# Three instruction orders written anew: a second attention core, the way to it, and a second convolution

## The chip, the core and the metric

The kernel runs on one core of a Trainium2 chip. The core has engines that work side by side, each through its own queue of instructions in order: TensorE (PE in the profile, its weight loads PEld), VectorE (DVE), ScalarE (ACT), GpSimd (POOL), and SyncE (SP), which here issues DMAs. They wait for each other by semaphores. The metric is the device time of one execution in microseconds; the time of a kernel is the median over its runs.

## The reference

Four layers act on x, of 2048 positions by 512 channels, each as x + f(layernorm(x)): A, B, A, B, with the same weights both times.

```python
def _A_ref(x, wqkv, wo):              # H = 32 heads of 16; window W = 8, dilation 2
    qkv = ... x @ wqkv ...
    idx = pos[:, None] - off[None, :]                  # off = 0, 2, .., 14
    logits = einsum("bhsd,bhswd->bhsw", q, kg) * scale # kg, vg: k and v at idx
    logits = where(mask, logits, -1e9)
    o = einsum("bhsw,bhswd->bhsd", softmax(logits), vg)
    return o.reshape(B, S, D) @ wo

def _B_ref(u, ...):                   # S4: a long convolution per channel
    P = exp(dt * A * l);  K = einsum("dn,dnl,dn->dl", Cc, P, dB).real
    y = irfft(rfft(pad(u)) * rfft(pad(K)))[:L]
    return y + u * Dskip
```

A is attention in which each position sees itself and seven others, at distances 2 to 14. B convolves each channel with a kernel K of full length, which is worked out from the parameters.

## The kernel before, in words

Position p*16 + a lies in partition p, row a: x is held as 128 partitions by 16 rows by 512 channels, so a distance of 2 positions is mostly a step of two rows, and a block b is four rows. The kernel goes through six stretches. The first (ORDERK, `k_gen`) works out K's table and, beside it, the first layer's norm and projections. The second is the first attention core (CORE0), the third the first convolution (ORDER0). Then come the three whose orders change: ORDERF, the end of the first convolution with the norm and the projections of the second A layer; CORE1, the second attention core; ORDER1, the second convolution.

What sets the order: the orders are strings written out by hand. Each token calls a function that records the instructions of one step on several engines. Under `manual_schedule`, TensorE, VectorE, ScalarE and SyncE get their instructions in the order of the tokens (DMAs of the ring loads are placed by the framework among SyncE's others). A token that stands earlier therefore stands earlier in the queue of each engine that it uses, and nothing overtakes it there.

The steps that the change and the prediction speak of:

* `differ(k)` (L1122 and on) ends a squaring of a table on TensorE: two matmuls in float32, each of two passes (L1129, L1130), that wait for ScalarE's squares `ws`. For k = 8, 9, 10 it first issues SQ_FILL[k] idle matmuls (L1128).
* ORDERF: `h` takes statistics of half a row on VectorE (L150), `H` of whole rows (L1553), `a` aggregates them (L1558), `p` makes 1/sqrt on ScalarE (L155, L156), `n` normalises a block of four rows (L197; D on VectorE, G half on GpSimd), `T` transposes it on TensorE (L273) into two halves that `E` copies out (L275; A on ScalarE, D on VectorE). `P` is one of 16 projections for k (four matmuls, L284, and ScalarE's copy L287), `Q` one for q (L223, L225). `x` and `e` copy a shifted part of k on VectorE (L297). `y`/`Y` (`i1`, in halves L901 or whole L897), `z`, `w` and `v` are the last steps of the convolution; `w` is 8 rows by 128 channels, `v` and `z` four rows. With the letter A ScalarE copies the sum of a `w`, `v` or `z` out and TensorE adds x by a matmul with the identity; with D VectorE adds x itself (L950). `S` gives half of the sums' buffers in PSUM to the projections.
* CORE1: `m` multiplies q by the windowed k for one of four parts ft of a block (`prod`, L344, VectorE; two buffers), `l` sums it over the channels of each head on TensorE (L352 for the first two blocks, L356 for the others), `x` takes the maximum, `e` subtracts it and takes the exponential, `r` the reciprocal of the sum, `n` normalises, `T` turns the first two blocks. `q` and `v` are projections (L223, L400). `P` multiplies a row's weights by v (`pav`, L469, VectorE; two buffers), `S` or `V` sums over the window on TensorE (L494, L484) and ScalarE copies the result (`oT`), `p` loads x into a PSUM buffer ahead (L501, ScalarE), `O` is the output projection (L511), with ScalarE's copy back to x and its sums for the next norm. `b` and `d` prepare that norm, `a` and `f` apply it to a row on VectorE or ScalarE. v is written row by row, even rows first; after v14 and v15 SyncE copies the even and the odd rows, shifted, for the windows (L405, L406). `w` loads a quarter of a table of the convolution.
* ORDER1: `U` is a first transform of u (TensorE, copied by VectorE or ScalarE, `a1s`), `u` a second one (ScalarE's copy `ub`, three buffers), `m` the product with the spectrum of K (VectorE, L871), `y`, `w` and `v` as above. A store of four rows (L1601) is issued when their last step is recorded.

In what follows m00 is token m of block 0, part 0; P0, S0, O0 are those of row 0; u14 is the fifteenth u, and so on.

Of the kernel before, what the change touches and what calls it, by code (L numbers as in the profile page):

```python
# [21 lines left out]
S = 2048  # L22
# [33 lines left out]
w010D  # L56
"""
ORDERF = """
yA h00 YA h01 v100A v110D h10 a0 z12A p0 z11A n0D h11 w001A w011A S a1 p1 T0 E01A z13A E00D n1G H2
P02 a2 P00 Q00 p2 T1 E10D E11D P01 P11 P12 n2D H3 a3 P13 T2 P10 E20D E21D P03 p3 P21 P22 n3D P23 T3  # L60
E30D E31A P20 x1
"""
ORDER1 = """
UA UD UA UD UA UA UD UA UD UD u u m m u u m m UA u UA UD m UA u u UD UA u m m u u m m u YD m u YA YA
m u yD m yA u u m m u w001A m m yA yA w000D YA yD yA YD w011D yA yD w010D yA yD yA v101A v103D v113A
v102D v112D v111D v110A v100A
"""

CORE0 = """
# [1 line left out]
nVPBeSOPSCd6wOPSwrPPnOSOSPPOSOPSbO9bFwEPAwVGaafOdSttDfOaHafa  # L71
"""
CORE1 = """
0mv12m3llmmqqqlqvlvmmvxvllmvevqrmvnllqqTvvmmlqlxmmvPPvvvvveqlmlqxmqSrnOSTpPPOlSeSrPOSOPSPPOSqlpO
SpmmOlOplnpPSxPeObbPdrpwVffaSfdOOPnVPPpfSpOSPpObafPSwOtppSdfwafwtaOa
"""
ROWS0 = (0, 2, 1, 3, 4, 5, 6, 7, 8, 9, 10, 11, 12, 13, 14, 15)
ROWS1 = (0, 2, 1, 3, 4, 5, 6, 7, 8, 9, 10, 11, 12, 13, 14, 15)
# [929 lines left out]
CH = 32  # L1008
NROW = 641
SQ_PE = 3  # L1010
SQ_FILL = {8: 13, 9: 6, 10: 2}


def k_gen(tc, nc, a_consts, ins, kd, la, x_v, lnst, zero, b_consts):
# [3 lines left out]
    with ExitStack() as ctx:  # L1018
# [102 lines left out]
        def differ(k):  # L1121
# [4 lines left out]
            re = pst.tile([P, 4 * P], F32, name="pt")  # L1126
            for _ in range(SQ_FILL.get(k, 0)):
                nc.tensor.matmul(re[:, 0:P], lhsT=ident32[:], rhs=nident32[:], start=True, stop=True)  # L1128
# [509 lines left out]
```

## Time and profile before

| | us |
|---|---|
| median of 3 runs | 397.38 (396.81 to 397.64) |
| profiled execution | 397.28 |
| its span | 395.5 |

| engine | busy us | share of the span |
|---|---|---|
| DVE | 377.5 | 95% |
| PE | 345.2 | 87% |
| ACT | 332.8 | 84% |
| PEld | 240.0 | 61% |
| POOL | 52.0 | 13% |

The profile is of one execution. A row of the timeline gives the start of a group of instructions in microseconds from the start of the span, its length, the engine, the line and the operation, the tile written and those read, the shapes and the count; in brackets stands how long the engine had been idle and what released it. A row of the chain gives start, length and what ran. A row by stretch gives, for each engine, its busy microseconds in the stretch, then TensorE's granted clock as a share of full speed, and the DMA engines' share and rate. The stretches: the way to the second core is about 235 to 263 us, the second core 261 to 350, the second convolution 350 to 392, then the last store.

### The profile page before, as it was taken

To read this page: it belongs to the slowest core of one execution; us is meant where nothing else is said; L and a number is where in the kernel's file an instruction comes from. 1 tells how busy PE (TensorE), PEld (TensorE's weight loads), DVE (VectorE), ACT (ScalarE), POOL (GpSimd) and SP (SyncE) were. 2 spreads that over 40 slices of the span, in tenths; PEclk is the share of its full clock that TensorE was granted. 3 is DMA by queue.
4 is the path that set the end of the run, shared out by engine and by line. 5 is a ranking of instruction groups with operands and counts; after the bars stand their busy time and mean duration, and the time that the engine had idled before them with its cause. 6 is when DMAs were issued, how large, how long until landed. Compare 5 with 4: busy or idle time off the path is not lost.

```text
span 395.5 us, 14987 instructions
## 1 busy us (share of the span) xinstructions
PE 345.2 (87%) x6551; PEld 240.0 (61%) x6598; DVE 377.5 (95%) x453; ACT 332.8 (84%) x594; POOL 52.0 (13%) x109
## 2 busy tenths in 40 slices
PE   3867667799999999889997889999999998887995
PEld 2225335485645677657887788543456666566885
DVE  6999999999999999999999989989999999989994
ACT  7999999899568789989999986674666899989974
POOL 9400100000370001002643500100000001000000
PEclk9999899999999999999999999999999999999999
DMA  7953811214125756394473907810153039505506
GB/s 224 388 159 41 80 53 32 64 29 92 53 50 144 196 169 179 97 364 169 166 247 125 323 15 209 317 58 0 49 153 95 3 106 325 163 2 163 162 10 207
DMA packets 63184, 54.17 MB, mean 137 GB/s; under 512 B 33035, under 2 KB 49968, under 8 KB 62864
## 3 DMA queue, kind: packets, MB, share of 16 engines
q1 hardware_dynamic: 60680, 46.60, 40.3%
q0 software_dynamic: 2432, 6.62, 4.7%
q8 instruction: 51, 0.84, 0.9%
q14 instruction: 13, 0.11, 0.1%
q10 hardware_dynamic: 8, 0.00, 0.0%
HBM read 30.15 MB, written 13.24 MB: 110 GB/s over the span
## 4 chain that ended last, share of the span: by engine, by line
DVE 35%; PE 33%; ACT 14%; issue 9%; DMA 6%; SPq 1%; POOL 1%; DVEq 0%; ACTq 0%; POOLq 0%
DVE pav L469 9%; PE pq L400 6%; DVE A_t L1161 4%; ACT a1s L814 4%; DVE prod L344 4%; DVE t L871 4%; PE pk L1327 4%; PE pq L223 3%; PE pp L284 3%; PE pp L1265 2%; DVE B_t L1161 2%; PE pq L511 2%; PE L L352 2%; PE po L494 2%; DMA pow_t<-pow_t 2%
## 5 line engine op out<-in xcount | busy, mean ns | idle before, releaser
L469 DVE TENSOR_TENSOR pav<-attn,v_ext 128x4096 bf16<-128x4096 bf16 (+1 forms) x34 | 72.0, 2163 | 0.3
L344 DVE TENSOR_TENSOR prod<-qT,kT_ext 128x4096 bf16<-128x4096 bf16 x29 | 65.2, 2288 | 0.7 <-PE L L352 0.5
L1161 DVE TENSOR_TENSOR A_t<-A_t,pow_t 128x1024 bf16<-128x1024 bf16 (+4 forms) x46 | 38.0, 872 | 0.4
L494 PEld LDWEIGHTS <-pav 64*128 64x128 bf16 x1664 | 26.5, 95 | 14.0 <-DVE pav L469 7.2
L494 PE MATMUL po<-ident,pav 64*128 64x64 bf16 x1664 | 29.1, 190 | 4.5 <-ACT oT L486 1.8
L511 PE MATMUL pq<-wop,oT 128*128 128x512 bf16 x113 | 30.7, 380 | 2.7 <-issue 1.3
L883 ACT CAST ub<-pb 128x1024 bf16<-128x1024 f32 x32 | 31.8, 1098 | 1.0 <-PE pb L832 1.0
L832 PE MATMUL pb<-a1s,w_sb 128*128 128x64 bf16 x768 | 27.8, 193 | 5.1 <-ACT ub L883 1.8
L400 PE MATMUL pq<-wv,xnT 128*128 128x512 bf16 x122 | 29.8, 379 | 0.2
L832 PEld LDWEIGHTS <-w_sb 128*128 128x128 bf16 x768 | 24.9, 98 | 7.7 <-issue 6.0
L814 ACT CAST a1s<-pb 128x1024 bf16<-128x1024 f32 x29 | 28.1, 1063 | 1.1 <-PE pb L825 1.1
L1265 PE MATMUL pp<-xnT,kT_ext 128*128 128x512 bf16 x88 | 23.0, 379 | 6.7 <-ACT xnT L1258 3.5
L402 ACT CAST v_ext<-pq 128x512 bf16<-128x512 f32 x32 | 18.6, 586 | 12.1 <-PE pq L400 11.9
L225 ACT CAST qT<-pq 128x512 bf16<-128x512 f32 x24 | 14.0, 584 | 12.8 <-PE pq L223 12.8
L1327 PE MATMUL pk<-B_t,A_t 128*64 128x84 bf16 (+1 forms) x512 | 23.3, 201 | 1.6 <-ACT kgs L1335 1.6
L1327 PEld LDWEIGHTS <-A_t 128*64 128x64 bf16 (+1 forms) x512 | 21.5, 103 | 5.3 <-issue 2.2
L814 DVE CAST a1s<-pb 128x1024 bf16<-128x1024 f32 x19 | 22.5, 1219 | 1.5 <-PE pb L825 1.4
L223 PE MATMUL pq<-xnT,kT_ext 128*128 128x512 bf16 x89 | 23.4, 380 | 0.4
L400 PEld LDWEIGHTS <-xnT 128*128 128x128 bf16 x128 | 11.7, 98 | 13.6 <-issue 1.3
L511 PEld LDWEIGHTS <-oT 128*128 128x128 bf16 x128 | 11.5, 98 | 12.7 <-ACT oT L496 2.2
L825 PE MATMUL pb<-F1c,xnT 128*64 128x128 bf16 x256 | 17.3, 219 | 1.9 <-ACT a1s L814 0.7
L1265 PEld LDWEIGHTS <-kT_ext 128*128 128x128 bf16 x96 | 8.5, 97 | 16.2 <-issue 8.4
(285 smaller groups left out, 918.2 us busy)
## 6 DMA issues: line engine op xcount, KB each, us to landing
w_sb<-w_dram SPq DMA_DIRECT2D x32, 256.0 KB, 5.6
w_dram<-xnT SPq DMA_DIRECT2D x1, 4096.0 KB
kf_ring<-kf_dram SPq DMA_DIRECT2D x13, 256.0 KB, 4.0
kf_ring<-kf_dram SPq DMA_DIRECT2D x26, 128.0 KB, 4.0
v_ext<-v_ext SPq DMA_DIRECT2D x4, 784.0 KB, 6.1
x_blk<-in_A_x_dram SPq DMA_DIRECT2D x4, 512.0 KB, 4.9
kT_ext<-in_A_wqkv_dram SPq DMA_DIRECT2D x4, 512.0 KB, 9.5
x_sb<-in_A_x_dram SPq DMA_DIRECT2D x4, 512.0 KB, 6.5
```

Of the source, the lines that this page charges most:

```text
L223: nc.tensor.matmul(pq[:], lhsT=self.wqk[:, dt, ft * P:(ft + 1) * P], rhs=self.xnT[:, dt, q * 512:(q + 1) * 512], start=(dt == 0), stop=(dt ...
L344: nc.vector.tensor_tensor(pr, self.qT[q][:, ft].unsqueeze(1).to_broadcast([P, W, 4, P]), kap, ALU.mult)
L400: nc.tensor.matmul(pp[:], lhsT=xnT[:, dt, a * P:(a + 1) * P], rhs=wv[:, dt, :], start=(dt == 0), stop=(dt == NDT - 1))
L469: nc.vector.tensor_tensor(pv[:, i], attn[:, n % 4].unsqueeze(2).to_broadcast([P, W, DH // parts, H]), vap, ALU.mult)
L494: nc.tensor.matmul(po[:, h, 0, i * nt + ft, :], lhsT=pvf[rows, i, w, ft * P:(ft + 1) * P], rhs=ident[rows, rows], start=(w == 0 and ft + i ...
L511: nc.tensor.matmul(pw[:], lhsT=oT[:, ftp, :], rhs=self.wo[:, ftp, :], start=False, stop=(ftp == NDT - 1), skip_group_check=ahead)
L814: (self.nc.scalar.copy if eng == "act" else self.nc.vector.tensor_copy)(dst, src)
L832: nc.tensor.matmul(p2[:, j, :], lhsT=self.w2[:, ec * EC + j, :], rhs=a1s[:, ec * EC + j, :], start=True, stop=True)
L883: nc.scalar.copy(ub[:], p2)
L1161: return lambda: nc.vector.tensor_tensor(*args)
L1265: nc.tensor.matmul(pps[kind, b, ft][:], lhsT=la.wqk[:, dt, c:c + P], rhs=la.xnT[:, dt, b * 512:(b + 1) * 512], start=(dt == 0), stop=(dt = ...
L1327: nc.tensor.matmul(o, lhsT=lhs, rhs=Bt[:, ri, c * CH + ql].rearrange("p b g -> p (b g)"), start=(not half and j % 4 == 0 and ri == 0), sto ...
```

## The change

Three strings are replaced and three numbers. ORDERF and CORE1 hold the same tokens as before in another order. In ORDER1, beside the order, w000 is copied out by ScalarE and no longer by VectorE (w000A for w000D), the last of the steps y, y15, is done in the whole form (Y), and the last steps v come in another order. SQ_FILL gets one idle matmul more for k = 8, two more for k = 9 and one more for k = 10.

```diff
 ORDERF = """
-yA h00 YA h01 v100A v110D h10 a0 z12A p0 z11A n0D h11 w001A w011A S a1 p1 T0 E01A z13A E00D n1G H2
-P02 a2 P00 Q00 p2 T1 E10D E11D P01 P11 P12 n2D H3 a3 P13 T2 P10 E20D E21D P03 p3 P21 P22 n3D P23 T3
-E30D E31A P20 x1
+yA YA h00 v100A h01 v110D h10 a0 z11A p0 w011A h11 n0D a1 z12A p1 S w001A T0 E01A z13A E00D P00 n1G
+H2 a2 P03 T1 Q00 E11D E10D p2 n2D P02 P01 H3 P10 P13 a3 P11 p3 T2 P12 E20D E21D n3D P23 P20 T3 E31A
+P22 x1 E30D P21
 """
 ORDER1 = """
-UA UD UA UD UA UA UD UA UD UD u u m m u u m m UA u UA UD m UA u u UD UA u m m u u m m u YD m u YA YA
-m u yD m yA u u m m u w001A m m yA yA w000D YA yD yA YD w011D yA yD w010D yA yD yA v101A v103D v113A
-v102D v112D v111D v110A v100A
+UA UD UA UD UA UA UD UA UD UD u u u UA UA m m UD UA u m UD u u UA m m u m m u u m m u u u YD YA m m
+YA u u yD m m yA yA yA u u m m m YA w000A w001A w010D yD yA YD yA yD yA yD YA w011D v101A v111D
+v102D v103D v113A v112D v110A v100A
 """
 CORE1 = """
-0mv12m3llmmqqqlqvlvmmvxvllmvevqrmvnllqqTvvmmlqlxmmvPPvvvvveqlmlqxmqSrnOSTpPPOlSeSrPOSOPSPPOSqlpO
-SpmmOlOplnpPSxPeObbPdrpwVffaSfdOOPnVPPpfSpOSPpObafPSwOtppSdfwafwtaOa
+0ml2vv1mmllq3mqqlvqqqmmxllmmevvrvvllnmmvqTvvlqxvlvvmmvPvvPellxrnqqqSTemmqSPOlPSOPSPOSOSPmOrpplSO
+OmbPndppllSfPxfOPSafebOVrPPppSOndpVwwfOPPSpOSpPbaOPfSdOppttSfafaaOww
 """
-SQ_FILL = {8: 13, 9: 6, 10: 2}
+SQ_FILL = {8: 14, 9: 8, 10: 3}
```

## The prediction

> **What bounds the kernel now.** I read the busy times by stretch first, then the chain that ended last, then the timelines of VectorE, ScalarE and TensorE in the second half, since the three orders act only behind 235 us.
>
> ```profile
> core 0: us, PE busy (x) PEld busy (x) DVE busy (x) ACT busy (x) POOL busy (x), PEclk, DMA share, GB/s
> ...
> 246.00:270.00 24.00, 23.45 (x155) 11.94 (x157) 21.41 (x45) 15.90 (x30) 1.68 (x2) 1.00 0.44 154
> 270.00:300.00 30.00, 29.73 (x296) 15.03 (x299) 30.00 (x16) 17.19 (x30) 0.00 (x0) 1.00 0.32 87
> 300.00:345.00 45.00, 40.55 (x1182) 28.99 (x1193) 44.51 (x38) 40.68 (x97) 1.04 (x1) 1.00 0.42 136
> ...
> 355.00:375.00 20.00, 16.35 (x470) 15.20 (x470) 19.87 (x18) 19.02 (x22) 0.00 (x0) 1.00 0.53 160
> 375.00:395.50 20.50, 15.42 (x470) 14.63 (x466) 15.35 (x16) 12.32 (x15) 0.00 (x0) 0.96 0.36 106
> ```
>
> The reader sees full engines: TensorE 23.45 of 24 us on the way to the second core, TensorE and VectorE together in that core's first half, VectorE in its second half with ScalarE close behind, VectorE and ScalarE in the convolution. The work stays the same but for one block, so an order can only take away the few waits that are left, or add some. The execution took 397.28 us, 1.78 around its span of 395.5; the median of the runs, 397.38, lies 0.1 higher. The sum is made against 397.28. About 0.2% (0.8 us) is what a measurement of this kernel can tell from no change.
>
> **Idle matmuls (SQ_FILL).**
>
> ```profile
> 30.60 3.06 PE L1128 MATMUL pt<-nident,ident 128*128 128x128 f32 x26
> 35.24 1.12 PE L1129 MATMUL pt<-ws,ident 128*128 128x512 f32 x2 [1.58 <-ACT ws L1114]
> ...
> 37.06 1.50 PE L1128 MATMUL pt<-nident,ident 128*128 128x128 f32 x12
> 41.38 1.27 PE L1129 MATMUL pt<-ws,ident 128*128 128x512 f32 x2 [2.81 <-ACT ws L1114]
> ...
> 44.15 1.06 PE L1128 MATMUL pt<-nident,ident 128*128 128x128 f32 x4
> 45.53 1.16 PE L1129 MATMUL pt<-ws,ident 128*128 128x512 f32 x2 [0.32 <-ACT ws L1114]
> ```
>
> ```profile
> 43.88 0.58 ACT L1149 CAST B_t<-pt 128x512 bf16<-128x512 f32 x1
> ```
>
> Thirteen calls are 26 passes in 3.06 us, 0.235 us each. One more at k=8 goes into a wait of 1.58 us, two more at k=9 (0.47) into one of 2.81. One more at k=10 takes 0.24 to 0.5 us of a wait of 0.32, so at most 0.2 sticks out, and the matmuls behind it feed copies that stand behind other ScalarE work. I take 0; bounds -0.3 and +0.2.
> Behind the wait of 2.81 us the matmuls are slow: the four passes from 41.38 are through at 44.15, in 2.77 us, those from 35.24 were through at 37.06, in 1.82. A shorter wait (2.34) could keep the clock up and give TensorE 0.95 us; but the reader of its result, ScalarE, is in its own queue until 43.88 and beyond, so I count nothing of it. The Trainium skill ("TensorE: Matmul & The Clock Gate", Part 1) has the clock halved after one idle window of some 3.4 us. Here it fell after 2.81 us with little work before, so the trace bears the rule out only roughly; by it the shorter wait would be safe, and that is the fourth case below.
>
> **The way to the second core (ORDERF).** The same 54 tokens in another order. Their price is when the first product (token m00, line 344) can start.
>
> ```profile
> 241.74 0.41 DVE L1558 BATCH_NORM_AGGREGATE ln_ag<-ln_bn 128x2 f32<-128x12 f32 x4
> ...
> 242.86 1.38 DVE L197 TENSOR_SCALAR xn<-x_sb,ln_rstd,ln_nb 128x512 bf16<-128x512 bf16 x4
> 244.15 1.40 DVE L150 BATCH_NORM_STATS2 ln_bn<-x_sb 128x6 f32<-128x256 bf16 x4
> ...
> 261.88 1.10 DVE L297 COPY kT_ext<-kT_ext 128x2032 bf16<-128x2032 bf16 x2 [0.35 <-ACT kT_ext L287]
> 263.02 2.29 DVE L344 TENSOR_TENSOR prod<-qT,kT_ext 128x4096 bf16<-128x4096 bf16 x1
> ...
> 268.68 8.90 DVE L344 TENSOR_TENSOR prod<-qT,kT_ext 128x4096 bf16<-128x4096 bf16 x4 [0.51 <-PE L L352]
> ```
>
> ```profile
> 246.26 1.00 ACT L275 COPY xnT<-pt 128x1024 bf16<-128x1024 bf16 x1
> ```
>
> ```profile
> 259.13 1.18 PE L273 MATMUL pt<-ident,xn 128*128 128x128 bf16 x16
> 260.14 3.40 PE L284 MATMUL pp<-xnT,kT_ext 128*128 128x512 bf16 x15
> ```
>
> ```profile
> 250.63 3.45 PE pp L284 x16
> ```
>
> h11, a set of statistics, now stands ahead of n0D on VectorE. a0 ends at 242.15, h11 takes 1.35, so the four normalisations of n0D end at 245.0, not 244.24; a1 ends at 245.3 and ScalarE's p1 at 245.75. Behind p1 ScalarE now has w001A's copy (0.95) before E01A, so E01A, the second half of the transposed block, runs 246.6 to 247.6, 0.35 later than in the row. TensorE is on T0 and z13A until 247.15, then on P00 (16 matmuls in 3.45 us, so 0.86 for a group of four), whose last two matmuls find E01A done. Before, it stood for E01A; so at P00 it has lost only some 0.15. Two small waits are new: P23 for E21D, 0.15 (p2 stands behind Q00's copy, which moves n2D, H3 and E21D back), and T3 for n3D, 0.1. P30 ended two groups after 260.14, at 261.87; now at about 262.2. P22 and P21 come between T3 and P30 and cover E30D and E31A. x2 waits for P21's copy at 262.0, e0 for P30's at 262.8, and m00 starts at about 263.2: **+0.15**. Bounds: 0, and +0.6 if E01A's whole delay and both waits count.
>
> **The second core (CORE1).** From m00 to 349.6 VectorE had one wait, the 0.51 us ahead of m02. l00 now follows m00 at once, so m02 finds its buffer free and this wait goes. In exchange other products wait for a buffer. From m00 to m20 VectorE has eight products of 2.2, 0.7 of small copies, a maximum (1.13) and n0 (0.6): 20.0 us, to 283.2. TensorE from P30 to l12 has 19 groups of 0.86, seven half sums of 0.49 and 1.3 of small ones and waits, 21.1, to 283.4. So m20 waits 0.2. In the same way m23 waits 0.15 for l21, and m30 0.15 for q30's copy. With the 0.15 of the start and without the 0.51, P0 starts at about 293.55, where it did, and P1 at 304.3 for 304.1:
>
> ```profile
> 268.08 0.98 PE L L352 x16
> ```
>
> ```profile
> 293.56 4.50 DVE L469 TENSOR_TENSOR pav<-attn,v_ext 128x4096 bf16<-128x4096 bf16 x2
> ...
> 304.10 13.30 DVE L469 TENSOR_TENSOR pav<-attn,v_ext 128x4096 bf16<-128x4096 bf16 x6
> ```
>
> ```profile
> L405 SPq DMA_DIRECT2D v_ext<-v_ext x2: 657/668/678, 283.6 to 296.3; - x2
> ...
> DMA to landing us min/median/max: 5.8/6.0/6.2
> ```
>
> **+0.2 so far**; bounds -0.35 (no new wait) and +0.9. v14 moves back: TensorE is through it at 284.9, so the two shifted copies of v issue at 285.5 and 286.2, not from 283.6, and land by 292.3. P0's slack falls from some 3 us to 1.2. On SyncE a further ring load (two transfers) now stands ahead of them; it has nothing to wait for.
> At the core's end ScalarE counts as much as VectorE:
>
> ```profile
> 324.88 1.09 ACT L501 CAST pq<-x_sb 128x512 f32<-128x512 bf16 x2
> ...
> 348.85 0.80 ACT L195 ACTIVATE xnT<-x_sb,ln_nb,ln_rstd 128x512 bf16<-128x512 bf16 x1
> ```
>
> ```profile
> 349.18 0.42 DVE L197 TENSOR_SCALAR xnT<-x_sb,ln_rstd,ln_nb 128x512 bf16<-128x512 bf16 x1
> ```
>
> Both end at 349.6. In the new order ScalarE is through p7 and p8 at about 322.8, and S7, behind P7 on VectorE, gives it oT7 only at 323.9: 1.05 us idle. b1's root waits for P9 on VectorE, 0.25 more. Before, at 325.97, it had done oT7, O7 and p9 too, 2.4 us of work; now that is done by 326.5. Part is caught up in later gaps: I add **+0.2**, bounds 0 and +1.3 (both waits in full).
>
> **The second convolution (ORDER1).** w000 goes from VectorE to ScalarE, with eight matmuls by the identity (0.45 us); y15 takes the whole form, 0.4 more on TensorE.
>
> ```profile
> 355.81 3.76 ACT L883 CAST ub<-pb 128x1024 bf16<-128x1024 f32 x4 [0.71 <-PE pb L832]
> ...
> 378.24 2.87 ACT L814 CAST xnT<-pb 128x1024 bf16<-128x1024 f32 x3
> ...
> 390.71 1.25 ACT L952 CAST x_sb<-pb 128x512 bf16<-128x512 f32 x2 [1.43 <-PE pb L948]
> ```
>
> ```profile
> 379.66 1.22 DVE L950 TENSOR_TENSOR x_sb<-pb,x_sb 128x1024 bf16<-128x1024 f32 x1
> ```
>
> ```profile
> 230.06 1.04 PE pb L901 x64
> 231.10 1.00 PE pb L897 x16
> ```
>
> From 355.81 to 381.1 ScalarE has 27 copies almost without a pause, 0.93 each. In the new order yA4, yA5 and yA6 stand ahead of u14 and u15, so u14 is its 24th and ends at 378.05, when VectorE has been through m13 since 377.3. m14 waits 0.75, and m15 ends at 380.35, not at 379.66. w010D cannot start before TensorE has passed w000A and w001A (24 matmuls, 1.4 us each), at 381.1: VectorE waits again. From y7 (376.3, behind yA5's copy) TensorE has one piece of 15.1 us: w000, w001, y7, y10 and y15 in the whole form (0.93), six in halves (0.52), w010, w011 and the eight last (1.1 a pair). It ends at 391.4, and v100A's copy at 392.05 against 391.96: **+0.1**. The block VectorE no longer has (1.13) is eaten by its two waits. Bounds: -1.1 (they vanish) and +0.7 (m15's shift reaches the end).
>
> **The stores.** w011D moves behind y15, so the two stores of rows 8 to 15 issue at about 388.3.
>
> ```profile
> 392.00:393.00 1.00, 0.00 (x0) 0.00 (x0) 0.00 (x0) 0.00 (x0) 0.00 (x0) 1.00 1.12 335
> ```
>
> ```profile
> L1601 SPq DMA_DIRECT2D out_dram<-x_sb x8: 372/373/1439, 384.4 to 392.0; - x8
> ...
> DMA to landing us min/median/max: 2.2/2.4/3.3
> ```
>
> Six stores of 262 KB then move from about 389.5. At 335 GB/s, the best row, that is 4.7 us, to 394.2, just when the last one (392.0 and 2.2) landed; at 300 it is 5.2. I add **+0.3**, bounds 0 and +1.
>
> **Sum**: 0 + 0.2 + 0.2 + 0.1 + 0.3 = +0.8, so 397.28 + 0.8 = 398.1.
>
> **Rivals.** Faster: VectorE bounds the convolution, with a block less. It decides if u14's copy ends before 377.3. Then -1.1 in place of +0.1 and no delay of the stores: 397.28 + 0.4 - 1.1 = 396.6, or 396.2 without the core's 0.4. For it: ScalarE is idle late (1.43 before 390.71). Against: the wait lies earlier, where it is full.
> Slower: ScalarE sets the end of the second core and catches nothing up. It decides once O7's statistics and p9 end later than 326.5. +1.3 in place of +0.2 is 399.2; 399.9 with the stores at their upper bound. For it: 40.68 of 45 busy. Against: up to 322.8 it has done some 0.7 us more than it had before. The shifted copies of v, should they land behind 293.55, would cost the same way, microsecond by microsecond; 1.2 us of slack speaks against it.
> Fourth: the added fills do keep the clock up between 42 and 46 us, and 0.3 of that arrives: 397.8.
>
> **How the numbers follow.** Forecast (+0.8; its own range 397.3 to 398.9) 0.50; slower 0.24; faster 0.21; fourth 0.05. Of the forecast's case some 0.20 lies beyond 398.2, 0.2% over the median, so slower is 0.24 + 0.20 = 0.44. Below 396.6 lies most of the faster case, 0.19. The rest, 0.37, is no change. The range goes from the faster case's 396.3 to the slower one's 399.7.
>
> **What would show it.** Right: m00 at 263.1 to 263.6; no wait ahead of m02; P1 near 304.3; ScalarE waiting about 1 us for S7 near 323; VectorE waiting near 378 (m14) and 380.5 (w010D); TensorE without a gap from 376 to 391; the last store landing behind 394.2. Wrong: VectorE unbroken until w010D, which is the faster case; a wait ahead of P0; any shift of VectorE before 60 us, which would come from the fills.

## The result and the profile after

The changed kernel takes 399.62 us (median of 6 runs, 398.67 to 401.59) against 397.20 (6 runs, 396.31 to 397.64). The ratio is 1.0068, with a 95% interval of 1.0049 to 1.0087, or +1.9 to +3.5 us. The forecast was 398.1, +0.8: the sign is right, but the loss is about three times the size.

The profiled execution took 399.53 us, with a span of 397.4; before it took 397.28, with 395.5. So 1.9 of its 2.25 us lie in the span, which the views show. The other 0.35 lie outside it: time less span is 2.07 to 2.16 in the six runs of the changed kernel and 2.06 to 2.15 in the six with its three orders alone, but 1.73 to 1.90 in those of the kernel before, and 1.74 to 1.90 where one part of the change stands alone. No trace shows what makes these 0.3 us.

By stretch, the changed kernel's rows for those of the prediction's first fence:

```profile
core 0: us, PE busy (x) PEld busy (x) DVE busy (x) ACT busy (x) POOL busy (x), PEclk, DMA share, GB/s
246.00:270.00 24.00, 23.70 (x163) 12.69 (x164) 21.08 (x44) 16.57 (x31) 1.68 (x2) 1.00 0.51 172
270.00:300.00 30.00, 29.71 (x307) 15.13 (x311) 29.42 (x17) 17.24 (x30) 0.00 (x0) 1.00 0.24 63
300.00:345.00 45.00, 39.69 (x1115) 28.09 (x1127) 44.16 (x35) 39.17 (x94) 2.94 (x1) 1.00 0.45 145
...
375.00:395.50 20.50, 17.68 (x496) 16.79 (x495) 16.12 (x16) 14.66 (x18) 0.00 (x0) 1.00 0.35 103
```

VectorE, full from 270 to 300 before, now waits 0.58 us there and 0.84 us from 300 to 345. The timelines tell more. First VectorE of the changed kernel, at the places where the prediction set its marks:

```profile
242.46 0.41 DVE L1558 BATCH_NORM_AGGREGATE ln_ag<-ln_bn 128x2 f32<-128x12 f32 x4
...
262.81 0.69 DVE L297 COPY kT_ext<-kT_ext 128x2032 bf16<-128x2032 bf16 x1 [1.76 <-ACT kT_ext L287]
...
264.00 2.29 DVE L344 TENSOR_TENSOR prod<-qT,kT_ext 128x4096 bf16<-128x4096 bf16 x1
...
284.72 4.49 DVE L344 TENSOR_TENSOR prod<-qT,kT_ext 128x4096 bf16<-128x4096 bf16 x2 [0.26 <-PE L L352]
...
294.85 4.49 DVE L469 TENSOR_TENSOR pav<-attn,v_ext 128x4096 bf16<-128x4096 bf16 x2
...
305.61 2.29 DVE L469 TENSOR_TENSOR pav<-attn,v_ext 128x4096 bf16<-128x4096 bf16 x1
...
350.87 0.45 DVE L197 TENSOR_SCALAR xnT<-x_sb,ln_rstd,ln_nb 128x512 bf16<-128x512 bf16 x1
...
379.70 2.36 DVE L871 TENSOR_TENSOR t<-ub,kf_ring 128x2048 bf16<-128x2048 bf16 x2 [0.41 <-ACT ub L883]
382.65 1.23 DVE L950 TENSOR_TENSOR x_sb<-pb,x_sb 128x1024 bf16<-128x1024 f32 x1 [0.58 <-PE pb L948]
```

The first row stands at 241.74 in the kernel before. VectorE's rows are as late from 235.01 on (234.29 before), which is ahead of ORDERF's first. So 0.72 us were lost before any of the three orders acts. The chain of starts then gives each part its share: m00 is 0.98 late (263.02 before), P0 1.29 (293.56), P1 1.51 (304.10), and the last a of the core ends 1.72 late (351.32 for 349.60). ScalarE's last copy, v100A, ends 1.93 late (391.96 before):

```profile
392.63 1.26 ACT L952 CAST x_sb<-pb 128x512 bf16<-128x512 f32 x2 [0.53 <-PE pb L948]
```

| part | predicted, us | this trace, us | alone: its ratio to the kernel before, times 397.2, us |
|---|---|---|---|
| idle matmuls | 0 (-0.3 to +0.2) | +0.72 | +0.8 (0.0 to +1.7) |
| ORDERF, to m00 | +0.15 | +0.26 | +0.5 (-0.1 to +1.1) |
| CORE1, m00 to P1 | about 0 | +0.53 | |
| CORE1, P1 to the end | +0.2 | +0.21 | whole of CORE1: +1.3 (+0.7 to +1.8) |
| ORDER1 | +0.1 | +0.21 | +0.2 (-0.3 to +0.7), with the stores |
| stores | +0.3 | 0 | |
| sum | +0.8 | +1.9 | all together: +2.7 (+1.9 to +3.5) |

The row CORE1, m00 to P1, and the row of the idle matmuls carry most of the miss.

Where the first 0.72 came from is seen on TensorE in the first attention core, whose order nobody touched. The kernel before:

```profile
172.42 0.73 PE L494 MATMUL po<-ident,pav 64*128 64x64 bf16 x38 [0.25 <-issue]
...
176.40 1.06 PE L484 MATMUL po<-ident,pav 128*128 128x128 bf16 x16
177.80 1.07 PE L484 MATMUL po<-ident,pav 128*128 128x128 bf16 x16 [0.34 <-issue]
```

and the kernel after, with the ScalarE copy that waits for this sum (it stood at 178.90):

```profile
172.46 0.84 PE L494 MATMUL po<-ident,pav 64*128 64x64 bf16 x46 [0.34 <-issue]
...
176.55 0.61 PE L484 MATMUL po<-ident,pav 128*128 128x128 bf16 x8
178.65 1.51 PE L484 MATMUL po<-ident,pav 128*128 128x128 bf16 x24 [1.49 <-issue]
```

```profile
180.20 0.59 ACT L486 CAST oT<-po 128x512 bf16<-128x512 f32 x1 [1.39 <-PE po L484]
```

"issue" means that TensorE waited for nothing that the profile shows. Of 32 equal matmuls 16 ran ahead of the stop, and now 8 do; at 172 us 46 come behind it, not 38. Both stops came eight matmuls earlier, as many as the four added idle calls issue. The stop is 1.15 longer; the copy is 1.3 late. TensorE runs out of work 0.30 sooner (177.16 for 177.46) and goes on 0.85 later. By 230 us part of it is eaten: VectorE is 1.30 late at 184 us, its wait of 0.43 us at 230.10 is gone, and it stands 0.75 late there.

```profile
230.10 1.23 DVE L950 TENSOR_TENSOR x_sb<-pb,x_sb 128x1024 bf16<-128x1024 f32 x1 [0.43 <-PE pb L948]
```

(This is the row of before.) From one stop to the next there are 128 matmuls, each with its weight load (46, 1, 4, 64, 1, 4 and 8 in the run with the idle matmuls alone; the changed kernel's trace lacks two of these records). And the profile's table of queues has one for instructions:

```profile
q8 instruction: 51, 0.84, 0.9%
```

51 packets with 0.84 MB, 16 KB each; the whole kernel before has 6598 weight loads, which is 51 times 128 and 70 more. So TensorE's program comes in pieces of 128 matmuls with their loads. In the changed kernel such a packet is found in the tenth of a microsecond from 176.1, while 16 transfers of table `w` keep the DMA engines at 386 GB/s (172 to 177). TensorE went on at 178.65.

### The profile page after: what moved, and what is told of

Read it like the earlier page. It is cut to its first block, busy times and chain, and to the rows that moved or that the text cites. A ratio compares the mean times of both kernels' runs of the same rounds, so it can differ in the third digit from the quotient of the medians.

```text
span 397.4 us, 14986 instructions
## 1 busy us (share of the span) xinstructions
PE 346.8 (87%) x6550; PEld 242.0 (61%) x6598; DVE 376.6 (95%) x452; ACT 333.8 (84%) x595; POOL 53.9 (14%) x109
## 4 chain that ended last, share of the span: by engine, by line
PE 47%; ACT 24%; DVE 20%; issue 5%; DMA 1%; POOLq 1%; POOL 1%; SPq 1%; DVEq 0%; ACTq 0%
ACT a1s L814 6%; PE pq L400 6%; PE pq L223 5%; ACT ub L883 5%; PE pk L1327 4%; DVE pav L469 4%; PE po L494 4%; PE pq L511 4%; PE pp L1265 4%; PE pp L284 3%; DVE A_t L1161 3%; DVE B_t L1161 3%; PE L L352 2%; PE L L356 2%; DVE prod L344 2%
## 5 line engine op out<-in xcount | busy, mean ns | idle before, releaser
L178 POOL TENSOR_TENSOR ln_rstd<-ln_rstd,ln_mh 128x4 f32<-128x4 f32 x2 | 4.0, 1996 | 112.6 <-DVE ln_rstd L177 112.6
```

## The experiments

All changes are made to the kernel before, unless said otherwise.

### Each part alone

```diff
-SQ_FILL = {8: 13, 9: 6, 10: 2}
+SQ_FILL = {8: 14, 9: 8, 10: 3}
```

> Only the idle matmuls are changed (14, 8, 3); all orders stay. Theory A: the eight idle matmuls more put TensorE's stop without a releaser near 177 us eight matmuls earlier and make it longer (0.34 us before, 1.49 after), because its program is being loaded while the transfers run at 370 GB/s: +0.7 to +1.2, so 397.9 to 398.4, with the shift arising at 177 to 181 us and nowhere before. Theory B: what the changed kernel lost in the first core is a chance of that run, and the prediction's 0 holds: 397.2, within 0.3, and the stop at 177 us is 0.2 to 0.5 us long.

397.80 us, ratio 1.0021 (0.9999 to 1.0043); single runs from 396.37 to 399.90. The stop of this kernel's TensorE:

```profile
172.34 0.84 PE L494 MATMUL po<-ident,pav 64*128 64x64 bf16 x46 [0.38 <-issue]
178.26 1.51 PE L484 MATMUL po<-ident,pav 128*128 128x128 bf16 x24 [1.22 <-issue]
```

The place is theory A's, and the long stop comes again. VectorE is 0.03 late at 183 us and 0.91 behind the stop, but only 0.37 at 230, where the wait of 0.43 is gone here too, and 0.30 at m00. The time lies between those of the two theories, and the interval just reaches 1: the place is shown, and that it costs, and how much, rests on this and on the next run.

The changed kernel with the idle matmuls of before:

```diff
-SQ_FILL = {8: 14, 9: 8, 10: 3}
+SQ_FILL = {8: 13, 9: 6, 10: 2}
```

> The changed kernel with 13, 6 and 2 idle matmuls: the three orders alone. Theory A: the orders cost what the trace shows behind 235 us, +1.2, so about 398.4, and VectorE reaches the first product of the second core with the shift of that order alone, 263.2 to 263.4. Theory B: the orders carry the whole loss: 399.6, within 0.4.

398.91 us, 1.0043 (1.0027 to 1.0059): +1.7, between the two theories. The stops are back in their old places (16 matmuls ahead), though that one was 0.89 us long here. m00 starts at 263.88, not at theory A's 263.2 to 263.4: in this execution, the longest of the six, VectorE was 0.61 late at the aggregation already (242.35), without the added matmuls. Of this 0.39 were there at 71 us, where nothing is changed. So a late start of ORDERF is not by itself a sign of the added matmuls. From the aggregation on m00 is 0.25 late, as in the changed kernel. By the medians the orders do not carry the whole loss; between 1.0068 and 1.0043 stand 1.0 us for eight matmuls.

The string ORDERF of the change, with nothing else:

> Only ORDERF. Prediction: the first product (m00) starts 0.15 later and all of it arrives: 397.35. The trace of the changed kernel read against the one before: +0.26, 397.5. Rival: the old CORE1 string, in which three products follow m00 ahead of l00, keeps its wait of 0.5 us ahead of m02 and takes the delay up in it: 397.2.

397.53 us, 1.0013 (0.9998 to 1.0028). In its trace the statistics are aggregated at 241.57 and m00 starts at 263.11, so they are 21.54 apart for 21.28 before: +0.26, the same as in the changed kernel. The interval reaches 1, so the time decides nothing; the rival is out in the trace: m02 keeps its 0.51 and starts 0.09 late, as m00 does.

The string CORE1 alone:

> Only CORE1. Prediction: +0.05 up to P1 and +0.2 at the core's end, 397.45 (without the +0.15 of ORDERF). The trace of the changed kernel: +0.5 up to P1 and +0.2 behind it, 397.9. Rival: the products' waits come from the later start alone, then 397.2 or less.

398.76 us, 1.0032 (1.0017 to 1.0046): +1.3 where +0.25 was predicted. The profiled execution, at 398.11, shows 0.8 of the loss; what the median has beyond that, no trace shows. VectorE of this kernel:

```profile
262.90 2.29 DVE L344 TENSOR_TENSOR prod<-qT,kT_ext 128x4096 bf16<-128x4096 bf16 x1
...
276.95 1.22 DVE L416 TENSOR_REDUCE mx<-L 128x128 bf16<-128x1024 f32 x1
278.26 4.49 DVE L344 TENSOR_TENSOR prod<-qT,kT_ext 128x4096 bf16<-128x4096 bf16 x2
282.67 0.69 DVE L447 TENSOR_TENSOR ex<-ex,rs 128x1024 bf16<-128x1024 bf16 x1
283.62 4.49 DVE L344 TENSOR_TENSOR prod<-qT,kT_ext 128x4096 bf16<-128x4096 bf16 x2 [0.26 <-PE L L352]
...
289.16 4.67 DVE L344 TENSOR_TENSOR prod<-qT,kT_ext 128x4096 bf16<-128x4096 bf16 x2
293.75 4.49 DVE L469 TENSOR_TENSOR pav<-attn,v_ext 128x4096 bf16<-128x4096 bf16 x2
...
299.28 0.68 DVE L447 TENSOR_TENSOR ex<-ex,rs 128x1024 bf16<-128x1024 bf16 x1
300.10 4.49 DVE L344 TENSOR_TENSOR prod<-qT,kT_ext 128x4096 bf16<-128x4096 bf16 x2
304.51 2.29 DVE L469 TENSOR_TENSOR pav<-attn,v_ext 128x4096 bf16<-128x4096 bf16 x1
```

The same stretch of the kernel before:

```profile
277.49 1.22 DVE L416 TENSOR_REDUCE mx<-L 128x128 bf16<-128x1024 f32 x1
278.62 4.49 DVE L344 TENSOR_TENSOR prod<-qT,kT_ext 128x4096 bf16<-128x4096 bf16 x2
283.02 0.69 DVE L447 TENSOR_TENSOR ex<-ex,rs 128x1024 bf16<-128x1024 bf16 x1
283.62 4.49 DVE L344 TENSOR_TENSOR prod<-qT,kT_ext 128x4096 bf16<-128x4096 bf16 x2
```

m00 starts 0.12 early, P1 0.41 late: +0.53, to the hundredth what the changed kernel has. From m00 to the maximum is 14.05 us for 14.47: m02's wait is worth 0.42. Then m12 starts 0.18 later behind the maximum than before (1.31 for 1.13), m20 0.35 later behind n0 (0.95 for 0.60), two products take 4.67 instead of 4.49 (m23, 0.18), and m30 comes 0.82 behind n1 where a 0.60 would do (0.22): 0.93 in all, for the 0.42 won. TensorE's rows show no gap from m00 to P1, in this kernel and in the one before. The rival (no loss from the front) is out.

The string ORDER1 alone:

> Only ORDER1. Prediction: +0.1 for the order and +0.3 for the stores: 397.6; a wait of VectorE of 0.75 us ahead of m14 and one ahead of w010D. From the runs so far (three orders together +1.7, ORDERF +0.5, CORE1 +1.27) nothing is left for it: 397.2. The prediction's faster rival: 396.1.

397.55 us, 1.0005 (0.9992 to 1.0018). Both waits are there, 0.41 and 0.58 us. It starts the convolution 0.63 early and ends its last copy 0.34 early: +0.29 in the trace. The faster rival is out.

### The second core's order, front and tail

The new order up to P1, the old behind it (the tail of the string is that of before without what has been issued):

```diff
-0mv12m3llmmqqqlqvlvmmvxvllmvevqrmvnllqqTvvmmlqlxmmvPPvvvvveqlmlqxmqSrnOSTpPPOlSeSrPOSOPSPPOSqlpO
+0ml2vv1mmllq3mqqlvqqqmmxllmmevvrvvllnmmvqTvvlqxvlvvmmvPvvPellxrnqqqSTemmqSPOpPOlSSrPOSOPSPPOSlpO
...
```

> The order before of the second core behind P1, the new one up to P1. Theory C: the new front alone costs what the trace of CORE1 alone shows up to P1, +0.5, by its three waits for TensorE: 397.7. Theory D: the old tail, with its slack on ScalarE and TensorE, takes that up: 397.2. Prediction: +0.05 without ORDERF, 397.25.

399.39 us, 1.0058 (1.0037 to 1.0079), slower than CORE1 whole. The trace has a wait of its own, that neither kernel has: VectorE stands 1.22 us for TensorE's sum S1, which in this mixture stands behind O0, O2 and l30. So its time says nothing of the front, though its trace has the front's 0.53 again (m00 at 262.52, P1 at 304.13). A second mixture has the cut at P6, where both orders have nearly the same steps left:

```diff
-0mv12m3llmmqqqlqvlvmmvxvllmvevqrmvnllqqTvvmmlqlxmmvPPvvvvveqlmlqxmqSrnOSTpPPOlSeSrPOSOPSPPOSqlpO
+0ml2vv1mmllq3mqqlvqqqmmxllmmevvrvvllnmmvqTvvlqxvlvvmmvPvvPellxrnqqqSTemmqSPOlPSOPSPOSOSPprPOSlpO
...
```

> The new order of the second core up to P6, the old one behind it, where both have the same steps in hand but for r2 and m32. Theory: only the front's loss, +0.5 (four waits for TensorE worth about 1.0 less the 0.5 of m02): 397.7. Rival: the tail's loss comes from the front's lateness and not from its own order: 398.4, as CORE1 alone.

398.05 us, 1.0020 (1.0007 to 1.0033). m00 starts 0.13 early, P1 0.40 late, and the last a 0.40 late: the front loses its 0.53, and the old tail adds nothing. The rival is out.

The old order up to P1, the new behind it:

```diff
-0mv12m3llmmqqqlqvlvmmvxvllmvevqrmvnllqqTvvmmlqlxmmvPPvvvvveqlmlqxmqSrnOSTpPPOlSeSrPOSOPSPPOSqlpO
-SpmmOlOplnpPSxPeObbPdrpwVffaSfdOOPnVPPpfSpOSPpObafPSwOtppSdfwafwtaOa
+0mv12m3llmmqqqlqvlvmmvxvllmvevqrmvnllqqTvvmmlqlxmmvPPvvvvveqlmlqxmqSrnOSTpPeqlPSOPSPOSOSPmOrplSO
+OmbPndppllSfPxfOPSafebOVrPPppSOndpVwwfOPPSpOSpPbaOPfSdOppttSfafaaOww
```

> The order before up to P1, the new one behind it. Prediction: ScalarE idle 1.05 us for S7 near 323 and +0.2: 397.4. Theory C: the wait of 0.33 us of d0 on VectorE for GpSimd's root, which the prediction did not name, arrives whole beside it: 397.6 to 397.8. Rival (ScalarE sets the end): 398.5.

398.17 us, 1.0019 (1.0005 to 1.0033). In the trace P1 starts 0.42 early and the last a starts 0.03 late: +0.45 (the profiled execution, at 397.34, is one of the shortest; the median lies above theory C's range). ScalarE stands 0.52 us for S7 (0.95 in CORE1 alone), and VectorE has the wait of theory C, and another one at the end (the second row is from CORE1 alone):

```profile
323.01 0.16 DVE L185 SCALAR_TENSOR_TENSOR ln_nb<-ln_s,ln_rstd 128x4 f32<-128x4 f32 x1 [0.33 <-POOL ln_rstd L178]
```

```profile
348.93 0.16 DVE L185 SCALAR_TENSOR_TENSOR ln_nb<-ln_ag,ln_rstd 128x3 f32<-128x3 f32 x1 [0.21 <-ACT ln_rstd L156]
```

The GpSimd root that d0 waits for, before and in CORE1 alone:

```profile
328.69 1.04 POOL L178 TENSOR_TENSOR ln_rstd<-ln_rstd,ln_mh 128x4 f32<-128x4 f32 x1 [80.36 <-DVE ln_msq L170]
```

```profile
320.70 2.94 POOL L178 TENSOR_TENSOR ln_rstd<-ln_rstd,ln_mh 128x4 f32<-128x4 f32 x1 [72.48 <-DVE ln_rstd L177]
```

It takes 2.94 us where it took 1.04. Before, it started 0.14 ahead of a product of VectorE's. Now it starts 0.24 behind one (320.46) and ends 0.90 behind that one's end (322.74). Then d0 moved behind P8:

```diff
-OmbPndppllSfPxfOPSafebOVrPPppSOndpVwwfOPPSpOSpPbaOPfSdOppttSfafaaOww
+OmbPnppllSPdfxfOPSafebOVrPPppSOndpVwwfOPPSpOSpPbaOPfSdOppttSfafaaOww
```

(the string of CORE1 alone on the minus side)

> CORE1 alone, with d0 (and f0 behind it) moved from ahead of P8 to behind it, so that VectorE need not wait for GpSimd's root. Theory: 0.3 of the tail's loss goes: 0.3 below CORE1 alone, 398.1. Rival: the wait is eaten later, since ScalarE (0.95 us idle for S7) sets the pace there: as CORE1 alone, 398.4. Rival: f0 and f1 on ScalarE come later and delay the end: 398.6 or more.

398.71 us, 1.0037 (1.0025 to 1.0048). The wait for GpSimd is gone, the tail is worse: from P1 to the last a the loss is 1.3 us, not 0.4. ScalarE and VectorE in this kernel:

```profile
325.25 1.52 ACT L195 ACTIVATE xnT<-x_sb,ln_nb,ln_rstd 128x512 bf16<-128x512 bf16 x2 [1.31 <-DVE ln_nb L185]
```

```profile
347.34 0.70 DVE L138 BATCH_NORM_STATS2 ln_bn<-pq 128x6 f32<-128x512 f32 x1 [0.79 <-PE pq L511]
```

ScalarE stands 1.31 us for d0 itself, and that delay reaches VectorE by way of O. The last rival holds: at both places that were tried somebody waits for d0.

### The place of the idle matmuls

```diff
-SQ_FILL = {8: 13, 9: 6, 10: 2}
+SQ_FILL = {8: 13, 9: 14, 10: 2}
```

> The kernel before with eight idle matmul calls more ahead of k = 9 alone (13, 14, 2), that is sixteen matmuls, 1.9 us in a wait of 2.8. Theory A (the place where TensorE's program breaks for the next load): the stop near 177 us comes sixteen matmuls earlier and ends no earlier, 2.4 to 2.7 us behind the start of the load: it is 0.9 us or more longer, +0.7 to +1.5, 397.9 to 398.7. Theory B (nothing of the fills arrives): 397.2, and a stop of 0.2 to 0.5 us.

398.15 us, 1.0022 (1.0005 to 1.0039). The stop comes sixteen matmuls earlier, just at the head of the sum (the row names a ScalarE operation, but in the kernel before the same sum starts at 176.40, ahead of that one at 177.33):

```profile
179.16 1.96 PE L484 MATMUL po<-ident,pav 128*128 128x128 bf16 x32 [1.55 <-ACT ln_rstd L156]
```

The load starts at 176.6, TensorE goes on 2.6 later. Theory A holds, though not with twice the cost of eight. VectorE is 1.75 late at the aggregation (243.49), but 0.85 were there at 21 us, ahead of the first idle matmul, where nothing is changed; the stretch with the stop is worth some 1.0.

```diff
-SQ_FILL = {8: 13, 9: 6, 10: 2}
+SQ_FILL = {8: 9, 9: 6, 10: 2}
```

> The kernel before with four idle calls fewer ahead of k = 8 (9, 6, 2): eight matmuls fewer. Theory A (the place where TensorE's program breaks): the stop near 177 us comes eight matmuls later and is gone or below 0.2 us, -0.1 to -0.4: 396.8 to 397.1. Theory B (nothing of the fills arrives): 397.2. Rival: the clock falls earlier than 42 us and that arrives: 397.4 to 398.2.

397.99 us, 1.0015 (1.0004 to 1.0026): slower, against theory A's sign. The stop near 177 is gone, as A has it (32 matmuls in one piece), though the load is early here too (174.4). But the breaks behind it have moved too, and one now falls into the first convolution. TensorE there:

```profile
228.30 0.20 PE L901 MATMUL pb<-Wp,t 64*128 64x64 bf16 x2 [1.13 <-issue]
```

In this execution (397.49) that stop lay in a wait that was there before (1.49 us ahead of the same group, for ScalarE), and VectorE ended only 0.15 late; what the median has beyond that, its trace does not show. The rival's time fits, but its clock does not: the mean granted clock is 1.00 from 30 to 48 us. With four calls fewer for k = 9 also:

```diff
-SQ_FILL = {8: 13, 9: 6, 10: 2}
+SQ_FILL = {8: 9, 9: 2, 10: 2}
```

> Also four calls fewer ahead of k = 9 (9, 2, 2): sixteen matmuls fewer. Theory A: no stop near 177 us, and the one near 172 us below 0.2: 396.7 to 397.0. Theory B: 397.2. Rival: with waits of 2.5 and 3.3 us the clock is low from 36 to 46 us, and TensorE becomes late for ScalarE: 397.5 to 398.5.

398.47 us, 1.0033 (1.0018 to 1.0048). Theory A's time is wrong, but its mechanism is at work: the same break, eight matmuls later, stops TensorE for 1.70 us, and the mean granted clock of the 5 us behind it is 0.66. The rival's clock is there too (0.72 from 36 to 42 us), but VectorE stands 0.13 early from 26 to 70 us, so nothing of it arrives there. VectorE is 0.24 late ahead of the stop and 2.1 late at 234:

```profile
229.25 0.21 PE L901 MATMUL pb<-Wp,t 64*128 64x64 bf16 x2 [1.70 <-issue]
```

```profile
230.00:235.00 5.00, 5.00 (x130) 4.61 (x128) 3.13 (x3) 1.92 (x3) 0.00 (x0) 0.66 0.03 7
```

As many matmuls more as in the change, in other waits:

```diff
-SQ_FILL = {8: 13, 9: 6, 10: 2}
+SQ_FILL = {4: 2, 7: 2, 8: 13, 9: 6, 10: 2}
```

> The kernel before with its 13, 6 and 2 idle calls as they are and four calls more in other waits: two ahead of k = 4, two ahead of k = 7 (0.47 us each in waits of 1.2). As many matmuls more as in the changed kernel, other cover, another clock between 35 and 46 us. Theory A (what counts is where TensorE's program breaks for the next load): the stops stand where they stand in the changed kernel, eight matmuls earlier than before, near 177 us 1.2 to 1.5 us long, and the time is that of the changed idle matmuls alone, 398.0 within 0.4. Theory B (what counts is the wait into which they are put): 397.2, a stop of 0.2 to 0.6 us.

397.90 us, 1.0012 (0.9993 to 1.0031). The break near 172 stands where it stands in the changed kernel (18 matmuls ahead, 46 behind):

```profile
172.41 0.85 PE L494 MATMUL po<-ident,pav 64*128 64x64 bf16 x46 [0.40 <-issue]
```

Near 177 this execution, at 397.31, had no stop: the load started at 174.4, sooner than in the kernels with a stop. The median is theory A's, the interval does not exclude theory B.

The load's start (the tenth of a microsecond in which the instruction packet stands in the DMA view) and the end of the stop, for all executions that have one near 177 us:

| kernel | load starts | TensorE goes on | between |
|---|---|---|---|
| before | 175.3 | 177.80 | 2.5 |
| ORDERF alone | 175.4 | 177.88 | 2.5 |
| CORE1 alone | 175.1 | 177.54 | 2.4 |
| ORDER1 alone | 174.9 | 177.40 | 2.5 |
| tail alone | 175.4 | 177.91 | 2.5 |
| front, cut at P6 | 175.1 | 177.79 | 2.7 |
| change without idle matmuls | 175.9 | 178.59 | 2.7 |
| idle matmuls alone | 175.7 | 178.26 | 2.6 |
| change | 176.1 | 178.65 | 2.6 |
| eight calls more at k = 9 | 176.6 | 179.16 | 2.6 |
| ORDER1, u14 first (below) | 175.1 | 177.71 | 2.6 |

TensorE goes on 2.4 to 2.7 us behind the load's start, whatever the kernel. The two breaks near 228 us agree: the loads start at 226.0 and 226.7, and TensorE goes on 2.3 and 2.6 later. So a stop has two parts: how soon TensorE reaches the break, which the count of matmuls sets, and when the load starts. What sets that start (173.6 to 176.6 over all traces) stays open. With the old place the stop near 177 is between nothing and 0.89 us long, with loads that start at 173.6 to 175.9. The transfers of `w` run at that time; that they make it late was not tried. In the two stops near 228 the DMA engines moved only some 30 GB/s from 227 to 228, and TensorE went on hardly sooner.

### Two single waits

l00 directly behind m00:

```diff
-0mv12m3llmmqqqlqvlvmmvxvllmvevqrmvnllqqTvvmmlqlxmmvPPvvvvveqlmlqxmqSrnOSTpPPOlSeSrPOSOPSPPOSqlpO
+0mlv12m3lmmqqqlqvlvmmvxvllmvevqrmvnllqqTvvmmlqlxmmvPPvvvvveqlmlqxmqSrnOSTpPPOlSeSrPOSOPSPPOSqlpO
...
```

> The kernel before with l00 moved ahead of v0 and of the two projections behind it, directly behind m00; nothing else. Theory (VectorE bounds the front, as the prediction took it): the 0.51 us ahead of m02 go and no other wait comes: 396.7. Rival (TensorE is full in the front, so that what is won at m02 is paid at m20 to m30): no change, 397.2, with new waits for TensorE that sum to 0.4 to 0.5.

397.73 us, 1.0010 (0.9991 to 1.0029). The wait for l00 goes, and another stands in its place at once:

```profile
269.05 0.29 DVE L297 COPY kT_ext<-kT_ext 128x508 bf16<-128x508 bf16 x1 [0.60 <-ACT kT_ext L287]
```

The shifted copy of k that stands ahead of m02 now waits for a projection that TensorE makes behind l00. The rival's result, one step earlier than it named.

ORDER1 as changed, u14 and u15 ahead of the three yA:

```diff
-YA u u yD m m yA yA yA u u m m m YA w000A w001A w010D yD yA YD yA yD yA yD YA w011D v101A v111D
+YA u u yD m m u u yA yA yA m m m YA w000A w001A w010D yD yA YD yA yD yA yD YA w011D v101A v111D
```

> ORDER1 as changed, but u14 and u15 ahead of yA4, yA5 and yA6, so that m14 does not wait. Prediction's reading (TensorE's one piece from 376 us on sets the end): m14's wait of 0.41 goes, w010D's grows by as much, 397.4 as ORDER1 alone. Rival (VectorE bounds): 0.4 less, 397.0.

399.21 us, 1.0049 (1.0032 to 1.0066), 1.7 slower than ORDER1 alone; both expectations miss. m14's wait goes, but ScalarE's copy of u14 has to wait for VectorE to free one of three buffers, TensorE's piece starts later by that, and VectorE pays at w010D:

```profile
374.93 2.15 ACT L883 CAST ub<-pb 128x1024 bf16<-128x1024 f32 x2 [1.11 <-DVE t L871]
```

```profile
381.88 1.23 DVE L950 TENSOR_TENSOR x_sb<-pb,x_sb 128x1024 bf16<-128x1024 f32 x1 [2.50 <-PE pb L948]
```

That TensorE's piece sets the end is borne out; that u14 could come earlier is not. No kernel tried beats the one before.

## Why the prediction was wrong, point by point

Two terms failed. The better measured one is CORE1 up to P1, priced at about 0: it costs 0.53 or 0.54 us in all six traces that have the new front, and CORE1 alone is +1.3 (+0.7 to +1.8). The other is the idle matmuls, priced at 0: there the mechanism is shown and the size is not.

**Idle matmuls: the step that failed by its mechanism.** It priced them by the waits into which they were put, and there the 0 was right: VectorE stands within 0.03 of before at 183 us with them alone. What was overlooked is that eight matmuls more move every later break of TensorE's program. One of the breaks stood in the middle of a sum that ScalarE waits for; the stop grew from 0.34 to 1.49 us and +0.7 arrived in that trace, outside the bound of +0.2. The row of before with 0.34 "issue" was in the trace and was not read. That the place moves is shown by the counts of matmuls in six kernels. Of the 1.15 us, 0.30 come from TensorE reaching the break sooner; the other 0.85 go with a load that starts 0.8 later, and why it did stays open. With the idle matmuls alone the trace kept 0.30 at m00, and the runs give +0.8 with 0 at the edge of the interval.

**The fourth rival** (the clock stays up at 42 to 46 us): in the changed kernel it did, and nothing of it arrived. It isn't the matmuls that decide it either. The float32 pairs behind the wait for k = 9, in the changed kernel (first row) and with the same idle matmuls alone:

```profile
42.49 1.02 PE L1130 MATMUL pt<-ws,nident 128*128 128x512 f32 x2
```

```profile
42.72 1.91 PE L1130 MATMUL pt<-ws,nident 128*128 128x512 f32 x2
```

Same wait of 2.37 us, other clock. The Trainium skill ("TensorE: Matmul & The Clock Gate", Part 1) calls its window free-running; that these two kernels, which are the same up to there, show both clocks behind one wait agrees with it.

**ORDERF**: +0.15 said, +0.26 measured in two traces. m00 came at 264.0 only because 0.72 was brought along.

**CORE1 to P1: mis-sized.** The mechanism was right: no wait ahead of m02, and waits of m20, m23 and m30 for TensorE. m23 (0.18 for 0.15) was right, m30 0.22 for 0.15, m20 0.35 for 0.2; m12's 0.18 was not named, and m02's wait was worth 0.42, not 0.51. All errors have one sign, and "about 0" became +0.53. TensorE was counted 0.2 behind VectorE at m20 (283.4 for 283.2) and measured 0.35 behind. It has no room in this stretch: its rows show no gap, and l00_first, which takes m02's wait for l00 away, has another of 0.60 at once. What one product gains, the next projection loses.

**CORE1's tail**: +0.2 said, +0.21 in the changed kernel, 0.38 in CORE1 alone and 0.45 with the old front. ScalarE's wait for S7 was there with 0.51 and 0.95 us for the 1.05 said. But d0's wait of 0.33 for GpSimd was not foreseen; it was priced as if a root took its 1.04 us anywhere. The Trainium skill ("SBUF — State Buffer", Who interferes with whom) says that a VectorE instruction with two inputs in SBUF contends with a GpSimd instruction that reads SBUF, and calls the pair of ports that they share an exclusive lock. The trace agrees as far as the product goes: started behind it, the root took 2.94 and ended 0.90 behind its end. But VectorE's multiplication of 128x1024 behind the product (322.66) took its usual 0.68 us while the root was still open.

**The slower rival** (ScalarE sets the core's end, 399.2 to 399.9) gave the time that was measured, by luck: the core's tail lost 0.2 in the changed kernel, not 1.3. The copies of v did no harm; P0 shows no wait.

**ORDER1**: m14 waits 0.41 for 0.75 said, w010D 0.58; TensorE has no gap in its rows behind 376.06; +0.21 for +0.1. The **faster rival** is out.

**The stores**: +0.3 said, 0 measured. The six stores run at the rate said, from 391.0 on, and their transfers end about 1.8 us behind ScalarE's last copy (393.89), as before behind 391.96:

```profile
391.00:392.00 1.00, 1.00 (x22) 1.00 (x20) 0.89 (x3) 0.48 (x1) 0.00 (x0) 1.00 1.06 319
...
395.00:396.00 1.00, 0.00 (x0) 0.00 (x0) 0.00 (x0) 0.00 (x0) 0.00 (x0) 0.65 0.73 220
```

The last store takes its 2.4 us from issue to landing in any case, and the others fit into that.

## What to carry to other kernels

An instruction added to a queue can cost more than its place: here it moved every later break of TensorE's program. So look in the trace for idle time with no releaser, count the instructions between two such places, and ask which of them moves into a critical piece of work. Where two engines are both full, a wait taken from one can come back as a wait for the other; price it at nothing before counting it as a gain. Look at what VectorE has just started when a short operation on GpSimd begins: here the same operation took 1.04 or 2.94 us.

## What the runs showed of the hardware

TensorE's program arrives in pieces of 16 KB, 128 matmuls with their weight loads. At a break TensorE went on 2.3 to 2.7 us behind the start of the load. Near 177 us, with the DMA engines at 390 GB/s, that made a stop of up to 1.55 us; near 228 us, with hardly a transfer from 227 to 228, stops of 1.13 and 1.70 us. The places are set by the number of matmuls ahead, idle ones 130 us earlier included. A stop of 1.70 us was followed by 5 us at a mean granted clock of 0.66. GpSimd's root of 128x4 elements took 1.04 us ahead of a VectorE product and 2.94 behind one.
